# One V quad beside each group of four K slots across sequence-pair boundaries, with the last rows' R, the transposing reads and the first bundle rearranged

## The chip, the cores and the metric

The kernel runs on 1 core of one Trainium2 chip. The metric is the device time of one execution in microseconds (us); lower is better. Most runs below were made in rounds, in which the kernel under test and the kernel before take turns on the same chip.

## The reference

A causal convolution with softmaxed taps feeds a channel mix with a gate:

```python
x = conv(x, softmax(weight))            # 8 x 4160 x 192, 7 taps, 8 heads of 24 channels
x_prev = x shifted by one token
xk = mu_k * x + (1 - mu_k) * x_prev
xr = mu_r * x + (1 - mu_r) * x_prev
k  = relu(xk @ w_k)                     # 192 -> 1024
v  = (k * k) @ w_v                      # 1024 -> 192
out = sigmoid(xr @ w_r) * v             # 192 -> 192 for the gate
```

## The kernel before

Two sequences at a time (a "pair", four in all) go through the same pipeline. Tokens are cut into steps of 512 and a tail of 64 (4160 = 8 x 512 + 64). A step's K product is eight "slots" of one PSUM tile each. Four slots are a "bundle", the unit of the main loop; the tail is a bundle of one slot. A "quad" is four 128-token tiles of V (or of R, the gate). All PSUM tiles come from one ring of four, so each new tile waits for the fourth one back to be read out.

```python
ring = ctx.enter_context(tc.tile_pool(name="ring", bufs=4, space=bass.MemoryType.PSUM))
...
quads = []                                   # (step, quad, bundle in which its V runs)
for s, (p, t0, L, n0, ns) in enumerate(steps):
    for j in range(max(1, L // 256)):
        quads.append((s, j, last_bundle[s] + 1 + j + (s == 0 or L == TAIL and p < NPAIR - 1)))
...
def v_tail(s):                               # R and V of a tail, in the two banks of one tile
    ps = ring.tile([P, 2, BANK], FP32, tag="k", name="ps_vt")
    r_mm(ps[:, 1, 0:D], s, 0)
    r_sb = two.tile([P, D], BF16, tag="r_tail", name="r_tail")
    nc.scalar.activation(out=r_sb, in_=ps[:, 1, 0:D], func=AF.Sigmoid)
    v_mm(ps[:, 0, 0:D], s, 0)
    nc.vector.tensor_tensor(out=o_sb, in0=ps[:, 0, 0:D], in1=r_sb, op=ALU.mult)
    ...
# schedule of convolutions, writes of y, transposing reads and x loads (g: group of token blocks)
    xs = range(fb - 9, fb - 9 + nx)          # convolutions of pairs 1 to 3
    at(late, xs[-1], y_write, g)
    at(late, xs[-1] + (1 if g == 4 else 2), y_read, g)      # transposing read, DRAM -> yT
    b = {4: 1, 5: 1, 6: 2, 7: 9, 8: 11, 9: 14}.get(g)       # x loads, on the GpSimd queue
    b = first_bundle[first_step[p]] + (-16, -12, -6, -3)[(g - 6) % 4] if b is None else b
    at(early, b, load_x, g)
...
for b in range(quads[-1][2] + 1):            # the main loop
    ns = bundles[b] if b < len(bundles) else ()
    run(early, b)
    if ns: k_section(ns)                     # K matmuls, TensorE
    for n in ns: k_relu(n)                   # relu, ScalarE
    run(first, b)                            # transposes on TensorE, pair 0 only
    run(vq, b)                               # V quads, TensorE
    run(mixes, b)                            # d, xk, xr, VectorE
    for n in ns[:3]: k_square(n)             # VectorE
    run(vo, b)                               # o_sb = V * R, VectorE; output
    run(xt, b)                               # convolution and its casts, R and its sigmoid, tails
    for n in ns[3:]: k_square(n)
    run(late, b)                             # y writes, transposing reads, on the SP queue
```

## Time and profile before

The kernel before took 466.4 to 469.4 us in the four runs beside which the change was first timed (median 466.45). In the list of engines, "busy" is a share of the whole span. In a timeline each row is: start in us, duration in us, engine, line of the kernel, operation, output and inputs, shapes, count, and in brackets how long the engine had been idle and what ended that. The chain that ended last, from the page of the kernel before, by engine:

```profile
PE 64%; DMA 8%; DVE 5%; ACT 3%; issue 2%; SPq 0%; DVEq 0%; ACTq 0%
```

Two thirds of it is TensorE; the rest is work that TensorE had to wait for, and DMA is the largest part of that rest. The profile also records the clock granted to TensorE; a "half-clock window" below is a stretch in which that record shows half the full clock (in the kernel before 3.41 us from 253.7 us). A "read" is a transposing read of y from DRAM, an "x load" a load of the input, issued by GpSimd.

### The profile page before, as it was taken

Reading aid. Unit: us, or ns where it says so; the run is one execution under the profiler, and the core shown is the slowest. Engines: PE = TensorE matmul, PEld = TensorE weight load, DVE = VectorE, ACT = ScalarE, POOL = GpSimd, SP = SyncE. Lnnn points to the kernel's source line nnn. Section 1 sums busy time; section 2 is a strip of 40 time slices with the busy share of each in tenths; the row PEclk is TensorE's granted clock in tenths of the full one; section 3 lists DMA queues with packets and bytes.
Section 4 is the critical chain, followed back from the end, with each engine's and each line's share of the span. In section 5 each row is a group of like instructions: output and inputs, shape, how many; then the busy total and the mean of one; then the engine's idle time right before and its main releaser. Section 6 shows DMA issues by size and latency. Waiting matters only on the chain.

```text
span 464.4 us, 9771 instructions
## 1 busy us (share of the span) xinstructions
PE 437.4 (94%) x3940; PEld 305.1 (66%) x3940; DVE 388.3 (84%) x699; ACT 354.1 (76%) x465; POOL 48.1 (10%) x70
## 2 busy tenths in 40 slices
PE   7789999899897999999987999999989799999996
PEld 3465776576755666676665666776666566677775
DVE  5799789788877899888877789889987799899982
ACT  3778888688757887888857778789886787777772
POOL 8550001012002010010202010001200000000000
PEclk9999999999999999999999999999999999999998
DMA  7998745995699596357948749359476456331123
GB/s 92 154 167 159 182 125 132 148 203 144 123 188 132 149 183 160 101 85 189 187 118 176 135 130 214 89 92 199 124 134 163 108 149 149 110 99 53 58 69 112
DMA packets 133183, 63.64 MB, mean 137 GB/s; under 512 B 84722, under 2 KB 132882, under 8 KB 133138
## 3 DMA queue, kind: packets, MB, share of 16 engines
q1 hardware_dynamic: 94834, 48.28, 40.5%
q0 software_dynamic: 38224, 14.68, 28.0%
q8 instruction: 31, 0.51, 0.4%
q14 instruction: 14, 0.11, 0.1%
q10 hardware_dynamic: 80, 0.05, 0.0%
HBM read 29.39 MB, written 36.99 MB: 143 GB/s over the span
## 4 chain that ended last, share of the span: by engine, by line
PE 64%; DMA 8%; DVE 5%; ACT 3%; issue 2%; SPq 0%; DVEq 0%; ACTq 0%
PE ps_v L488 28%; PE ps_k L406 27%; DMA yT<-y_dram 6%; PE ps_r L484 3%; PE ps_r L483 3%; DMA xb<-in_x_dram 2%; PE ps_c L250 2%; ACT k_sb L446 2%; DVE k L465 2%; DVE o_sb L515 1%; PE ps_vt L488 1%; DVE d L345 1%; DVE xk L384 1%; DVE xk L387 0%; PE ps_k L434 0%
## 5 line engine op out<-in xcount | busy, mean ns | idle before, releaser
L446 ACT ACTIVATE k_sb<-ps_k 128x1024 bf16<-128x1024 f32 x260 | 245.7, 1033 | 19.0 <-PE ps_k L406 12.3
L406 PE MATMUL ps_k<-xk,wk 64*128 64x512 bf16 (+3 forms) x1056 | 192.3, 375 | 5.7 <-DVE xk L387 2.1
L488 PE MATMUL ps_v<-wv,k 128*128 128x192 bf16 x2048 | 179.4, 246 | 3.4 <-DVE o_sb L515 2.8
L488 PEld LDWEIGHTS <-k 128*128 128x128 bf16 x2048 | 170.7, 98 | 17.2 <-issue 3.7
L465 DVE TENSOR_TENSOR k<-k_sb 128x1024 bf16<-128x1024 bf16 x256 | 168.6, 686 | 12.3 <-ACT k_sb L446 11.1
L406 PEld LDWEIGHTS <-wk 64*128 64x128 bf16 (+1 forms) x1056 | 66.7, 96 | 107.1 <-issue 60.8
L515 DVE TENSOR_TENSOR o_sb<-ps_v,r_sb 128x768 f32<-128x768 f32 x64 | 61.2, 957 | 31.6 <-PE ps_v L488 31.6
L505 ACT ACTIVATE r_sb<-ps_r 128x768 bf16<-128x768 f32 x64 | 52.9, 828 | 28.0 <-PE ps_r L484 28.0
L286 ACT CAST y<-ps_c 120x480 bf16<-120x480 f32 (+6 forms) x84 | 38.6, 521 | 41.4 <-PE ps_c L250 41.4
L122 POOL DMA_DIRECT2D xb<-in_x_dram x36 | 32.2, 899 | 178.4 <-PE ps_k L406 98.6
L483 PE MATMUL ps_r<-wr,xr 128*128 128x192 bf16 x256 | 47.8, 248 | 0.3 <-ACT k_sb L446 0.3
L484 PE MATMUL ps_r<-wr,xr 128*128 128x192 bf16 x256 | 47.9, 248 | 0.0
L387 DVE TENSOR_TENSOR xr<-xr,yT 128x1024 bf16<-128x1024 bf16 (+1 forms) x66 | 36.2, 549 | 2.3
L387 DVE TENSOR_TENSOR xk<-xk,yT 128x1024 bf16<-128x1024 bf16 (+1 forms) x66 | 36.2, 549 | 2.3
L345 DVE TENSOR_TENSOR d<-yT 128x1536 bf16<-128x1536 bf16 (+2 forms) x37 | 31.6, 854 | 6.8 <-DMA yT<-y_dram 6.7
L250 PE MATMUL ps_c<-xb,toe 128*128 128x480 bf16 (+4 forms) x144 | 31.6, 322 | 1.6 <-DVE toe L224 0.9
L384 DVE TENSOR_SCALAR xk<-d,mu 128x1024 bf16<-128x1024 bf16 (+1 forms) x66 | 28.2, 427 | 1.2
L484 PEld LDWEIGHTS <-xr 128*128 128x128 bf16 x256 | 25.2, 98 | 4.1 <-issue 0.5
L289 ACT CAST y<-ps_c 120x480 bf16<-120x480 f32 (+6 forms) x45 | 20.7, 508 | 8.9 <-PE ps_c L250 8.9
L483 PEld LDWEIGHTS <-xr 128*128 128x128 bf16 x256 | 25.1, 98 | 3.6
L384 DVE TENSOR_SCALAR xr<-d,mu 128x1024 bf16<-128x1024 bf16 (+1 forms) x66 | 26.9, 408 | 0.0
L250 PEld LDWEIGHTS <-toe 128*128 128x128 bf16 x144 | 12.8, 98 | 4.4 <-DVE toe L224 1.6
(57 smaller groups left out, 79.6 us busy)
## 6 DMA issues: line engine op xcount, KB each, us to landing
out_dram<-o_sb SPq DMA_DIRECT2D x62, 384.0 KB, 2.9
y_dram<-y SPq DMA_DIRECT2D x10, 900.0 KB, 7.3
xb<-in_x_dram POOLq DMA_DIRECT2D x14, 480.0 KB, 8.4
xb<-in_x_dram POOLq DMA_DIRECT2D x6, 432.0 KB, 7.6
xb<-in_x_dram POOLq DMA_DIRECT2D x10, 192.0 KB, 6.3
y_dram<-y SPq DMA_DIRECT2D x3, 450.0 KB, 4.1
y_dram<-y SPq DMA_DIRECT2D x1, 810.0 KB, 6.3
xb<-in_x_dram POOLq DMA_DIRECT2D x2, 384.0 KB, 7.0
```

The source lines that it names most:

```text
L250: nc.tensor.matmul(out=ps[:, :, :, i * G : (i + 1) * G], lhsT=toe[:, h, :], rhs=xbs[g][:, :nb, :, h * G : (h + 1) * G], start=True, stop=True,
L286: copy(out=yh[:, :, :, c0 : c0 + n], in_=ps[:BLK, :, :, 0:n])
L384: nc.vector.tensor_scalar(out=o, in0=d[:, sl, :L], scalar1=mu[:, i, part : part + 1], scalar2=None, op0=ALU.mult)
L387: nc.vector.tensor_tensor(out=o, in0=o, in1=yT[:, sl, c0 : c0 + L], op=ALU.add)
L406: nc.tensor.matmul(out=ps[:, i, f * L : (f + 1) * L], lhsT=wk[r, 0 if hi else 1, fs], rhs=xk[r, i if hi else 2, :L], start=start and f == ...
L446: nc.scalar.activation(out=k_sb, in_=ps.rearrange("p a b -> p (a b)"), func=AF.Relu)
L465: nc.vector.tensor_tensor(out=o, in0=i, in1=i, op=ALU.mult)
L483: nc.tensor.matmul(out=o, lhsT=hi, rhs=wr[:, 0, :], start=True, stop=False)
L484: nc.tensor.matmul(out=o, lhsT=lo, rhs=wlo, start=False, stop=True)
L488: nc.tensor.matmul(out=o, lhsT=k2s[s][:, f, t * P : (t + 1) * P], rhs=wv[:, f, :], start=(f == 0), stop=(f == NF - 1),)
L505: nc.scalar.activation(out=r_sbs[s, j], in_=ps, func=AF.Sigmoid)
L515: nc.vector.tensor_tensor(out=o_sb.rearrange("p (b t) d -> p b (t d)", b=2), in0=v_ps.pop((s, j)), in1=r_sbs.pop((s, j)), op=ALU.mult,)
```

## The change

The intent: where one pair hands over to the next, give each group of four K slots one V quad again, so that the evictions of K on ScalarE and the products on VectorE stay spread out. The tail's R moves a bundle ahead of its V. The transposing reads (and what feeds them) come one bundle sooner, and the first bundle runs in two halves so that the transposes for the second step start sooner.

```diff
@@ k_section: works for a part of a bundle
+        h = len(ns) // 2
-        for n in ns[:2]:            (hi and lo halves of the first two slots, then of the others)
+        for n in ns[:h]:
...
@@ where each V quad goes
     quads = []
+    vb = 1
     for s, (p, t0, L, n0, ns) in enumerate(steps):
-        for j in range(max(1, L // 256)):
-            quads.append((s, j, last_bundle[s] + 1 + j + (s == 0 or L == TAIL and p < NPAIR - 1)))
+        for j in range(L // 256):
+            vb = max(vb, last_bundle[s]) + 1
+            if p < NPAIR - 1 and vb < len(bundles) and len(bundles[vb]) == 1:
+                vb += 1
+            quads.append((s, j, vb))
+        if L == TAIL:
+            quads.append((s, 0, vb))
@@ the tail's R, a tile of its own
+    def r_tail(s):
+        ps = ring.tile([P, 2, BANK], FP32, tag="k", name="ps_rt")
+        r_mm(ps[:, 0, 0:D], s, 0)
+        r_sbs[s, 0] = two.tile([P, D], BF16, tag="r_tail", name="r_tail")
+        nc.scalar.activation(out=r_sbs[s, 0], in_=ps[:, 0, 0:D], func=AF.Sigmoid)
...
+            at(xt, vb - 1, r_tail, s)
             at(xt, vb, v_tail, s)
@@ convolutions, writes, reads and x loads of pairs 1 to 3
-            xs = range(fb - 9, fb - 9 + nx)
+            xs = range(fb - 10, fb - 10 + nx)
-            b = {4: 1, 5: 1, 6: 2, 7: 9, 8: 11, 9: 14}.get(g)
-            b = first_bundle[first_step[p]] + (-16, -12, -6, -3)[(g - 6) % 4] if b is None else b
+            b = {4: 1, 5: 1, 6: 2, 7: 5, 8: 10, 9: 13}.get(g)
+            b = first_bundle[first_step[p]] + (-17, -13, -7, -4)[(g - 6) % 4] if b is None else b
@@ main loop: bundle 0 in halves
-            if ns:
-                k_section(ns)
-            for n in ns:
-                k_relu(n)
-            run(first, b)
+            for part in (ns[:2], ns[2:]) if b == 0 else (ns,):
+                if part:
+                    k_section(part)
+                for n in part:
+                    k_relu(n)
+                if part[:1] == ns[:1]:
+                    run(first, b)
```

More of the change, by code (lines that the diff above doesn't have):

```diff
@@ L418, in k_section @@
             return k_mm_tail(ns[0], steps[s][0])
-        for n in ns[:2]:
+        h = len(ns) // 2
+        for n in ns[:h]:
             k_mm(n, True, True)
-        for n in ns[:2]:
+        for n in ns[:h]:
             k_mm(n, False, False)
-        for n in ns[2:]:
+        for n in ns[h:]:
             k_mm(n, False, True)
-        for n in ns[2:]:
+        for n in ns[h:]:
             k_mm(n, True, False)
@@ L531, in v_tail @@
         ps = ring.tile([P, 2, BANK], FP32, tag="k", name="ps_vt")
-        r_mm(ps[:, 1, 0:D], s, 0)
-        r_sb = two.tile([P, D], BF16, tag="r_tail", name="r_tail")
-        nc.scalar.activation(out=r_sb, in_=ps[:, 1, 0:D], func=AF.Sigmoid)
         v_mm(ps[:, 0, 0:D], s, 0)
         o_sb = two.tile([P, D], FP32, tag="o_tail", name="o_tail")
-        nc.vector.tensor_tensor(out=o_sb, in0=ps[:, 0, 0:D], in1=r_sb, op=ALU.mult)
+        nc.vector.tensor_tensor(out=o_sb, in0=ps[:, 0, 0:D], in1=r_sbs.pop((s, 0)), op=ALU.mult)
         for i in range(2):
```

## The prediction

> **What bounds the kernel now.** I read the page first, for the busy shares and the clock.
>
> ```profile
> PE 437.4 (94%) x3940; PEld 305.1 (66%) x3940; DVE 388.3 (84%) x699; ACT 354.1 (76%) x465; POOL 48.1 (10%) x70
> PEclk9999999999999999999999999999999999999998
> ```
>
> TensorE leads, VectorE is ten points behind, and the clock is nearly whole. Then the timeline of TensorE alone, to see whether there are gaps and where. A plain bundle, here one of pair 0:
>
> ```profile
> 97.20 2.96 PE L406 MATMUL ps_k<-xk,wk 128*128 128x512 bf16 x16
> 100.00 2.80 PE L488 MATMUL ps_v<-wv,k 128*128 128x192 bf16 x32
> 102.64 0.57 PE L250 MATMUL ps_c<-xb,toe 128*128 128x480 bf16 x2
> ...
> 103.70 2.96 PE L406 MATMUL ps_k<-xk,wk 128*128 128x512 bf16 x16
> ```
>
> By its starts a bundle is K 2.80, V 2.64, convolution 0.41, R 0.66 us: 6.50 us without a gap. Here only less TensorE work would help, and the change removes none. The gaps lie elsewhere: at the start, in one bundle near 90 us, and at the three places where one pair of sequences hands over to the next. The first hand-over, from the last full bundle of pair 0 to the second step of pair 1:
>
> ```profile
> 116.72 3.00 PE L406 MATMUL ps_k<-xk,wk 128*128 128x256 bf16 x32
> 119.55 2.80 PE L488 MATMUL ps_v<-wv,k 128*128 128x192 bf16 x32
> ...
> 125.42 1.07 PE L434 MATMUL ps_k<-tail,wk 128*128 128x128 bf16 x16 [1.34 <-DVE o_sb L515]
> 126.32 5.44 PE L488 MATMUL ps_v<-wv,k 128*128 128x192 bf16 x64
> 131.60 0.57 PE L250 MATMUL ps_c<-xb,toe 128*128 128x480 bf16 x2
> 132.00 2.96 PE L406 MATMUL ps_k<-xk,wk 128*128 128x512 bf16 x16
> ...
> 138.13 1.36 PE L406 MATMUL ps_k<-xk,wk 64*128 64x512 bf16 x6 [0.48 <-ACT y L286]
> ...
> 143.02 0.82 PE L488 MATMUL ps_vt<-wv,k2t 128*128 128x192 bf16 x8 [2.72 <-ACT r_tail L534]
> ...
> 144.34 2.97 PE L406 MATMUL ps_k<-xk,wk 128*128 128x512 bf16 x16
> ```
>
> Two V quads run back to back beside the tiny tail K, then eight K slots come with no V beside them. Eight evictions of about 1 us on ScalarE then cannot hide behind 5.6 us of K. The list of waits shows which of these repeat:
>
> ```profile
> PE ps_vt L488 <- ACT r_tail L534: 8.6, 4, 2.7
> DVE d L345 <- DMA yT<-y_dram: 6.7, 4, 2.8
> ```
>
> Three r_tail waits are 2.72 us each: the tail's R is issued, its sigmoid queues on ScalarE behind four relus and the casts, and the tail's V stands behind it.
>
> Last, the timeline around the second hand-over and at the start:
>
> ```profile
> 20.12 2.98 PE L406 MATMUL ps_k<-xk,wk 128*128 128x512 bf16 x16 [2.14 <-DVE xk L387]
> ...
> 231.25 0.96 DVE L345 TENSOR_TENSOR d<-yT 128x1536 bf16<-128x1536 bf16 x1 [2.02 <-DMA yT<-y_dram]
> ...
> 236.92 2.84 PE L488 MATMUL ps_v<-wv,k 128*128 128x192 bf16 x32 [1.57 <-DVE o_sb L515]
> ...
> 254.72 4.12 PE L406 MATMUL ps_k<-xk,wk 128*128 128x512 bf16 x16
> ```
>
> The late transposing read delays d on VectorE, so the product that frees V's PSUM tile is late, and TensorE waits 1.57 us. The K after the r_tail gap took 4.12 us instead of 2.97.
>
> [...]its clock record has one half-clock window of 3.41 us from 253.7 us, right after the second r_tail gap, and none after the other two, which have the same gap. [...]r_tail's sigmoid, ready near 140.3, starts at 142.47 after casts emitted before it. [...]the transposing read issued at 50.08 with no x load behind it landed after 6.7 us; those at 76.03, 110.80, 221.87 and 333.42, each with an x load issued about 1 us later, landed after 9.4, 8.9, 9.4 and 9.0 us.
>
> **Part 1, V quads and the tail's R across hand-overs.** Nothing is added or removed; one VectorE/ScalarE instruction each way at most. Computing the new lists by hand: the tail's bundle gets no V, the next two bundles of the new pair get one V each, and V of the tail follows in the second, with its R already in the first. TensorE's work from the K of the last full bundle to the K four bundles on is three bundles with convolution, 3 x 6.50 = 19.5, plus tail K 0.90, one more convolution 0.41, tail R 0.16, tail V 0.66: 21.6 us. Measured by starts, the three hand-overs take 144.34 - 116.72 = 27.6, 254.72 - 227.79 = 26.9, 365.43 - 339.34 = 26.1 us. Idle: 6.0 + 5.3 + 4.5 = 15.8 us. The half-clock K adds 4.12 - 2.97 = 1.15, not inside these. So 16.9 us is the most that can be won here.
>
> What stays. In the new order the first thing in the tail's bundle that needs V's PSUM tile is an R, 2.83 + 2.64 + 0.41 + 0.90 + 0.41 = 7.2 us after the K. VectorE ends that product in the first hand-over at 125.36, 8.6 us after K, of which 0.28 was a DMA wait: 8.4 - 7.2 = 1.2 us stay. That bundle carries four mixing groups (two steps and a tail) on VectorE. In the second: 236.86 - 2.02 - 227.79 = 7.05; in the third the same: nothing stays. ScalarE in the last full bundle and the tail's bundle has 3.77 + 1.02 + 1.02 + 1.02 + 0.83 = 7.7 us against TensorE's 7.9, and its sigmoid then sits just before the fourth K slot of the next bundle: I leave 0.7 us there in the second and third, 0.1 in the first. Residue 1.3 + 0.7 + 0.7 = 2.7. Gain 16.9 - 2.7 = **14.2 us**.
>
> **Part 2, everything for the transpose a bundle sooner.** Convolution, write, read and x loads of pairs 1 to 3 all move by one bundle (some 6.5 us), so the waits of 0.28, 2.02 and 1.65 us on the hand-over reads go; that is already in part 1. The first x load of pair 1 moves from bundle 9 to 5: it leaves the side of the read in bundle 8 (d waited 2.80 us, TensorE 2.06 at 91.13) and comes to stand beside the read of bundle 4. By the landing times above that read becomes 9.4 instead of 6.7 us, 59.5 instead of 56.8; d started at 57.03, so it waits about 2.4, and 0.26 of slack follows. TensorE waits about 2.0 near 63 instead of 2.06 near 91. Net **0.3 us** won.
>
> **Part 3, first bundle in halves.** The transposes for step 1 come after two K slots instead of four, so 1.4 us sooner by 2.9/2 of K. VectorE's chain from there (copies, d, mix) is what K at 20.12 waits for (2.14 us), and ScalarE, busy without a gap from 21.53 to 31.8, starts as much sooner. The halves now take one slot after the other with two more switches between 128 and 64 rows: **1.2 us** won.
>
> **Part 4, the end.** The last tail's V waits 0.42 us for its sigmoid; now gone: **0.4 us**.
>
> Sum: 14.2 + 0.3 + 1.2 + 0.4 = 16.1. I keep back 0.4 for small waits not listed. 466.5 - 15.7 = **450.8 us**, 3.4% less.
>
> **Rivals.** (a) VectorE takes over at the hand-overs. Its work there is, in the first, some 8.4 + 0.7 + 5.6 + 7.1 = 21.8 us (from the rows of d, xk, xr, square 0.69, product 0.96), as much as TensorE's 21.6; in the others 7.1 + 0.7 + 5.6 + 7.1 = 20.5. For it: these are sums without waits[...]. Against: it comes out of the last bundle only 0.7 us late. It would cost 1 to 1.5 us more per hand-over: about 455. (b) The ring of four PSUM tiles: R of the tail now takes its own tile, and the fourth K slot behind it waits for its sigmoid. ScalarE in that bundle has 3.77 + 1.02 + 0.83 + 0.45 = 6.1 against TensorE's 6.7. If it lags, 0.5 each: 452. (c) The moved x load: if the read beside it lands later still, or the early bundles, where ScalarE is full, lose what the halves win: 452.5. (d) All waits vanish: 466.5 - 18.5 = 448.
>
> **Range and chances.** The gain of part 1 is bounded above by counted idle time, below by (a) with (b) and (c) together, about 456. I say 447.5 to 455.5. The 2% line is at 457.4; to miss it more than 40% of the idle must come back. Faster 0.90, within 2% 0.09, slower 0.01.
>
> **What the new profile should show.** No V wait on r_tail; K starts four bundles apart at hand-overs 22 to 23 us; first hand-over slowest, an R waiting about 1 us for a product; no half-clock window there; d waiting for a transposing read once, near 57 to 60 us, followed by a K wait near 62; K of the second bundle near 18.9 instead of 20.12; plain bundles still 6.1 to 6.5. I am wrong if plain bundles lengthen, or if VectorE shows waits of over 2 us on TensorE at each hand-over while V sits in order.

## The result, and the profile after

The changed kernel took 449.63, 456.72, 450.66 and 455.44 us: median 453.05. The ratio to the kernel before is 0.9676, 95% interval 0.9597 to 0.9755: faster. A ratio here is the mean time of one kernel's fast runs over that of the other's fast runs of the same rounds, so it is not quite the ratio of the medians. The profile fell on the 449.63 us run. Busy shares and the chain, from its page:

```profile
PE 430.4 (96%) x3877; PEld 304.4 (68%) x3940; DVE 387.9 (87%) x699; ACT 354.1 (79%) x465; POOL 48.2 (11%) x70
...
PE 81%; DVE 8%; ACT 4%; DMA 4%; issue 2%; SPq 0%; DVEq 0%; ACTq 0%
```

The work is the same (VectorE, ScalarE and the weight loads within 1 us; 63 matmul records are missing from this trace, so its PE time reads low). The chain is now 81% TensorE instead of 64%. The first hand-over on TensorE, from its timeline:

```profile
115.14 3.00 PE L406 MATMUL ps_k<-xk,wk 128*128 128x256 bf16 x32
117.97 2.80 PE L495 MATMUL ps_v<-wv,k 128*128 128x192 bf16 x32
...
121.01 1.06 PE L435 MATMUL ps_k<-tail,wk 128*128 128x128 bf16 x16
...
123.53 0.24 PE L490 MATMUL ps_r<-wr,xr 128*128 128x192 bf16 x1 [1.05 <-DVE o_sb L522]
...
126.99 2.80 PE L495 MATMUL ps_v<-wv,k 128*128 128x192 bf16 x32
...
136.78 0.82 PE L495 MATMUL ps_vt<-wv,k2t 128*128 128x192 bf16 x8
...
138.10 2.96 PE L406 MATMUL ps_k<-xk,wk 128*128 128x512 bf16 x15
```

From K to K it takes 138.10 - 115.14 = 22.96 us, where it took 27.62. The 2.72 us wait of the tail's V is gone, and one wait is left: an R for the product of the last V. The other two hand-overs take 21.99 and 21.98 us with no wait that the timeline marks. The second bundle's K, from the same timeline:

```profile
18.88 2.98 PE L406 MATMUL ps_k<-xk,wk 128*128 128x512 bf16 x15 [1.13 <-DVE xk L387]
```

It was at 20.12 with a 2.14 us wait. And in bundle 6 and 7, from the timelines of VectorE and TensorE:

```profile
57.52 0.96 DVE L345 TENSOR_TENSOR d<-yT 128x1536 bf16<-128x1536 bf16 x1 [1.66 <-DMA yT<-y_dram]
...
63.19 2.53 PE L406 MATMUL ps_k<-xk,wk 128*128 128x512 bf16 x14 [1.21 <-DVE o_sb L522]
```

It comes in place of one in the kernel before:

```profile
91.13 2.53 PE L406 MATMUL ps_k<-xk,wk 128*128 128x512 bf16 x14 [2.06 <-DVE o_sb L515]
```

That one belonged to the read in bundle 8, beside which the x load stood before; the new one belongs to the read in bundle 4, beside which it stands now. One more thing is new, and the profile of one run cannot show it: the runs fall into two sets, near 450 and near 455 to 457 us. The first set is what the prediction worked out; many of the experiments went into the second.

### The profile page after: what moved, and what is told of

The parts are those of the page before. It is cut to its first block, busy times and chain, and to the rows that moved or that the text cites. A ratio compares the mean times of both kernels' runs of the same rounds, so it can differ in the third digit from the quotient of the medians.

```text
span 447.8 us, 9705 instructions
## 1 busy us (share of the span) xinstructions
PE 430.4 (96%) x3877; PEld 304.4 (68%) x3940; DVE 387.9 (87%) x699; ACT 354.1 (79%) x465; POOL 48.2 (11%) x70
## 4 chain that ended last, share of the span: by engine, by line
PE 81%; DVE 8%; ACT 4%; DMA 4%; issue 2%; SPq 0%; DVEq 0%; ACTq 0%
PE ps_v L495 35%; PE ps_k L406 34%; PE ps_r L490 4%; PE ps_r L491 4%; PE ps_c L250 4%; DMA yT<-y_dram 4%; DVE k L466 2%; ACT y L286 2%; DVE o_sb L522 1%; ACT k_sb L447 1%; DVE d L345 1%; DVE xk L387 1%; DMA w_raw<-in_weight_dram 1%; DVE xk L384 1%; ACT y L289 1%
## 5 line engine op out<-in xcount | busy, mean ns | idle before, releaser
L406 PE MATMUL ps_k<-xk,wk 64*128 64x512 bf16 (+3 forms) x994 | 187.7, 373 | 7.3 <-DVE o_sb L522 1.6
L495 PEld LDWEIGHTS <-k 128*128 128x128 bf16 x2048 | 170.9, 98 | 14.9 <-issue 0.7
L250 PEld LDWEIGHTS <-toe 128*128 128x128 bf16 x144 | 12.7, 98 | 2.9 <-DVE toe L224 1.5
```

What stands on the lines that cost most here:

```text
L250: nc.tensor.matmul(out=ps[:, :, :, i * G : (i + 1) * G], lhsT=toe[:, h, :], rhs=xbs[g][:, :nb, :, h * G : (h + 1) * G], start=True, stop=True,
L406: nc.tensor.matmul(out=ps[:, i, f * L : (f + 1) * L], lhsT=wk[r, 0 if hi else 1, fs], rhs=xk[r, i if hi else 2, :L], start=start and f == ...
L495: nc.tensor.matmul(out=o, lhsT=k2s[s][:, f, t * P : (t + 1) * P], rhs=wv[:, f, :], start=(f == 0), stop=(f == NF - 1),)
```

## The experiments

Each experiment tells what it changes against the changed kernel, or against the kernel named. The "quiet" runs are those near the fastest; the runs of the second set are called slow here. The record has a state "slow" of its own, for runs over 1.5% above the fastest of their kernel; it falls on some runs of the second set only (456.72 in the first rounds, 458.34 in again, 456.83 in tail_xr, three in no_halves), and the ratios leave those out. All results were correct. Twelve kernels ran, on four chips, and the kernel before itself ran from 463.1 to 472.1 us beside them, so small differences are read from runs of one call or from the traces.

### The two sets of runs: again, no_halves, load_b6, tail_xr

These four ran in one call on one chip. **again** is the changed kernel without an edit.

> The changed kernel itself once more, because its four runs went from 449.6 to 456.7 us where those of the kernel before lie within 0.2 us but for one. I expect 449.5 to 456.8 again, two or three of the runs near 450 and the others near 455. Theory V1 (half-clock windows[...]): a slow run has a granted clock some 0.004 to 0.008 under 0.998. Theory V2 (data for the first bundles comes late in some runs): slow runs may have the full clock and a long wait of a convolution or of K in the first 40 us.

Measured: 449.36, 456.05, 456.06, 458.34, 450.12, 449.96 us; ratio 0.9667 (0.9598 to 0.9736). The spread is real and as expected; the profile fell on a quiet run. Two of the slow runs, 456.05 and 456.06 us, had a granted clock of 0.995. Over their 454 us that is at most 2.3 us of lost clock (an estimate from these two numbers), and they are some 6 us longer than the quiet ones: the clock alone can't make the second set.

**no_halves:**

```diff
-            for part in (ns[:2], ns[2:]) if b == 0 else (ns,):
+            for part in (ns,):
```

> The changed kernel with the first bundle whole again. Undoing the halves should cost 1.2 us beside a fast run of the changed kernel: 450.8 to 451.0 us, with the K of the second bundle near 20.1 us again. On the spread: V2 says that the halves brought the kernel closer to the x loads of the start (a convolution waits 0.25 us for its load at 22.7 us, which it did not before), so without them the runs should lie within 1 us; V1 says the spread stays as wide as with them.

Measured: 450.60, 454.85, 458.80, 459.04, 458.21, 455.81 us; ratio 0.9775 (0.9719 to 0.9831), unclear at 2%. Its quietest run is 1.2 us over that of again. The spread stays, so theory V2 (late data at the start, brought on by the halves) falls.

**load_b6:**

```diff
-            b = {4: 1, 5: 1, 6: 2, 7: 5, 8: 10, 9: 13}.get(g)
+            b = {4: 1, 5: 1, 6: 2, 7: 6, 8: 10, 9: 13}.get(g)
```

> The first x load of pair 1 in bundle 6 instead of 5, away from the transposing reads of bundles 4 and 8. My theory says the x load beside a read makes it land 2.2 to 2.7 us later: then the wait of K at 63.2 us (1.21 us) goes and nothing comes at 89: 448.3 to 448.6 us fast. The rival, that the read of bundle 4 is late of itself (writes of y and other traffic), leaves the 1.2 us wait where it is: 449.6.

Measured: 448.40, 449.13, 448.51, 448.92, 448.39, 448.72 us; ratio 0.959 (0.9545 to 0.9634). One number moved, and the second set of runs is gone. The K wait at 63 us is gone too. VectorE's d, which waited 1.66 us for the read in the changed kernel, now shows no wait:

```profile
55.76 0.96 DVE L345 TENSOR_TENSOR d<-yT 128x1536 bf16<-128x1536 bf16 x1
```

So the x load in bundle 5 makes the slow runs, and V1 (clock windows alone, at random) falls as their main cause.

**tail_xr:**

```diff
-        rb = fb - 1 if L == TAIL else fb
+        rb = fb - 1 if L == TAIL and p == NPAIR - 1 else fb
```

> The mixing of the tail's xr (three VectorE operations, 0.83 us) in the tail's own bundle instead of the one before, for pairs 0 to 2. My theory: R in the first hand-over waits 1.05 us because VectorE has too much in the bundle before the tail, so 0.8 of it goes: 448.8 us fast, the other two hand-overs unchanged. Rival: the product there waits for V or for a relu, then nothing changes: 449.6.

Measured: 454.95, 449.47, 449.46, 456.83, 449.53, 455.67 us; ratio 0.9657 (0.959 to 0.9724). Here the profile fell on a slow run (454.95 us; the record's state is fast). Its timelines of VectorE and TensorE in bundles 6 and 7:

```profile
61.53 0.96 DVE L345 TENSOR_TENSOR d<-yT 128x1536 bf16<-128x1536 bf16 x1 [5.82 <-DMA yT<-y_dram]
...
63.81 0.60 PE L406 MATMUL ps_k<-xk,wk 128*128 128x512 bf16 x2 [2.20 <-DVE xk L387]
...
67.20 3.37 PE L406 MATMUL ps_k<-xk,wk 128*128 128x512 bf16 x11 [2.79 <-DVE o_sb L522]
```

The transposing read came 4 us later than in the quiet trace (5.82 us of wait against 1.66), TensorE waits twice, and the clock record shows 6.8 us of half clock from 65.0 us. The parts of DMA issued between 48 and 66 us, with the time from issue to landing at the end of the line, first for the quiet changed kernel:

```profile
xb<-in_x_dram POOLq DMA_DIRECT2D x2, 480.0 KB, 9.4
yT<-y_dram SPq DMA_TRANSPOSE x1, 8.7
```

and for the slow run of tail_xr:

```profile
xb<-in_x_dram POOLq DMA_DIRECT2D x2, 480.0 KB, 11.6
yT<-y_dram SPq DMA_TRANSPOSE x1, 12.8
```

and for load_b6, where the x load comes a bundle later:

```profile
xb<-in_x_dram POOLq DMA_DIRECT2D x2, 480.0 KB, 6.6
yT<-y_dram SPq DMA_TRANSPOSE x1, 6.2
```

Counting the DMA packets of the traces by the microsecond in which they end shows what happens in between (256-byte packets belong to the read, 384-byte packets to the x load):

```
us                     50   51   52   53   54   55   56   57   58   59   60   61
changed, quiet  read    6 1012  995 1134  374   71    8    0    0    0    0    0
                x       0    0    0    0  306  444  491  492  504  261   62    0
tail_xr, slow   read  155  866  533  223  273  280  275  285  278  276  155    1
                x       0    0  122  219  272  272  270  275  275  279  255  191
```

In both, the read is issued at 48.7 to 48.8 us and the x load 0.64 us behind it. In the quiet run the x packets begin at 54, when the read is nearly done. In the slow run they begin at 52, and from then on the read gets some 280 packets a microsecond instead of 1000 to 1130. There read and x load end nearly the same number of packets in each microsecond from 54 to 59 (273 to 285 against 270 to 279), though a packet of the one is 256 bytes and of the other 384.

As to the tail's xr: in this trace the first hand-over takes 143.44 - 121.34 = 22.10 us instead of 22.96, as expected, but the three quiet runs are hardly faster than those of again (449.49 against 449.81 us on average, where 0.8 was expected). Whether the quiet runs waited longer at the read is not known, since none was profiled; **best** below settles the part about xr.

### The overlap made certain: load_b4

```diff
-            at(early, b, x_tile, g, nc.vector)
-            at(early, b, load_x, g)
+            tb, b = (xt, 4) if g == 7 else (early, b)
+            at(tb, b, x_tile, g, nc.vector)
+            at(tb, b, load_x, g)
```

> The changed kernel with the first x load issued about two us sooner, just before the transposing read of bundle 4 instead of just behind it. If slow runs come from x packets starting while that read is still running, nearly every run should now be slow: the read's packets take about 10 us instead of 5.3, d waits 4 to 6 us, 454 to 458 us, no run near 450. Rival (the spread is chance in the memory or the clock and not this overlap): the same mix as before, with some runs near 450.

Measured: 457.87, 455.57, 457.03, 455.73, 457.87, 459.15 us; ratio 0.9804 (0.9763 to 0.9846), unclear at 2%. All six runs are slow. The edit did less than intended: GpSimd still waited and issued the load only 0.04 us behind the read instead of 0.64. That was enough: the x packets begin at 51.3 us, ahead of the read's at 52.5. VectorE's timeline, and the DMA issued between 48 and 66 us:

```profile
63.16 0.96 DVE L345 TENSOR_TENSOR d<-yT 128x1536 bf16<-128x1536 bf16 x1 [6.97 <-DMA yT<-y_dram]
```

```profile
yT<-y_dram SPq DMA_TRANSPOSE x1, 14.0
```

So the overlap is the cause of the second set: all six runs are slow where it is made certain, none where the load is moved away. (No slow run of the changed kernel without an edit was profiled; that its slow runs are like the one of tail_xr is inferred.)

In this case much goes with how close behind the read the x load is issued. In the traces there are four reads with an x load issued 0.04 to 0.34 us behind them, this one and three in b6_old_quads below; in all four the x packets start inside the read (here even ahead of its first packet), which then lands after 10.8 to 17.4 us. At 0.64 us, where the change put the first x load, they do so in one profiled run of four (tail_xr; not in those of the changed kernel, again and no_halves). At 0.66 to 2.4 us, some 90 reads in the 14 profiles, they never start more than 1.3 us before 95% of the read's packets have ended.

What remains open is why, with the same issue times, the x packets start at 52 in one run and at 54 in another; no run here tests a cause.

### The same move in the kernel before: before_b6

```diff
-            b = {4: 1, 5: 1, 6: 2, 7: 9, 8: 11, 9: 14}.get(g)      (in the kernel before)
+            b = {4: 1, 5: 1, 6: 2, 7: 6, 8: 11, 9: 14}.get(g)
```

> The kernel before with one number changed: the first x load of pair 1 in bundle 6 instead of 9, so that it stands beside no transposing read. Theory (x packets that start while the read is still running slow it, and how early they start varies from run to run): the 2.06 us K wait near 91 us goes, 464.2 us where the kernel before has 466.4; its runs still spread by 2 to 6 us, because the reads at its hand-overs, with an x load behind each, have no slack (d waits 0.28, 2.02 and 1.65 us even in a quiet run). Rival, that only the read in bundle 8 varies: all runs within 1 us.

Measured: 462.54 to 466.03 us, median 464.79 in 12 runs; the kernel before beside it 463.55 to 472.13. Ratio 0.9951 (0.9924 to 0.9978): the same at 2%. In the trace the bundle that took 8.73 us (88.47 to 97.20) takes 6.67, so the 2.06 us of the theory are there. The spread narrows from 5.3 us (the fast runs; 8.6 with one run in the record's slow state) to 3.5. The profiled run (465.18 us) has half-clock windows at 20.7 and 252.8 us; the bundles in which they fall take 0.9 and 1.1 us more than in traces without. In the kernel before the time goes with the clock: over the runs beside all the experiments, six with a granted clock of 1.000 took 463.1 to 464.1 us, eleven with 0.985 took 468.4 to 470.0 us. So such windows may well make up its spread, and a read that varies, as in the theory, is not shown for it; no experiment tells the two apart.

### The parts one by one, from load_b6

With the disturbance gone, the parts can be undone singly. The reference point is load_b6: 448.62 us, spread 0.7. Hand-overs are K to K as above.

**b6_old_quads** (V quads by the old formula; the tail's R still ahead, the reads still early):

```diff
-        for j in range(L // 256):
-            vb = max(vb, last_bundle[s]) + 1
-            ...
+        for j in range(max(1, L // 256)):
+            quads.append((s, j, last_bundle[s] + 1 + j + (s == 0 or L == TAIL and p < NPAIR - 1)))
```

> From load_b6, V quads placed as before (two V beside the tail's K), while the tail's R stays a bundle ahead and the reads stay early. My prediction put all of the hand-over gain in one sum. Splitting it: of the idle 6.0 + 5.3 + 4.5 us of before, the tail's sigmoid makes 2.9 each, late reads 0.3, 1.6 and 1.2; left for the V order are 2.8, 0.8 and 0.4, against 1.4, 0.4 and 0.4 that load_b6 still has. So 448.6 + 1.8 = 450.4 us. Rival, that the V order carries most of the gain, as the name of the change says: 455 or more.

Measured: 453.69, 454.57, 453.45, 455.33, 453.93 us; ratio 0.9718 (0.9676 to 0.976). The order of V is worth 5.3 us, not the 1.8 I had split off. TensorE at the first hand-over:

```profile
123.56 5.44 PE L489 MATMUL ps_v<-wv,k 128*128 128x192 bf16 x64
129.25 2.96 PE L406 MATMUL ps_k<-xk,wk 128*128 128x512 bf16 x16
133.54 0.59 PE L406 MATMUL ps_k<-xk,wk 128*128 128x512 bf16 x2 [0.59 <-ACT k_sb L447]
...
137.51 0.82 PE L489 MATMUL ps_vt<-wv,k2t 128*128 128x192 bf16 x8
```

Eight K slots without a V run into the relus (at 133.54), as the prediction read it from the kernel before. The hand-overs take 25.08, 22.54 and 22.54 us (load_b6: 22.97, 21.98, 21.99), together 3.2 us more, and the bundles behind them lose another 1.1, 0.3 and 0.3. The remaining 0.3 us is at the start of the profiled run, where a convolution waited 1.31 us for its x load (0.38 in load_b6), and is no part of the change. The loss behind the hand-overs was in none of my sums: I had counted only up to the fourth K. And 0.8 of the 1.1 us is not the V order itself: the old order also moved the x loads closer behind the reads, the read issued at 131.01 landed after 17.4 us with an x load 0.29 us behind it, d waited 1.53 us for it, and the K at 154.08 waited for the product behind d. That leaves some 4.2 us for the V order.

**b6_r_beside** (the tail's R back beside its V, in one tile; the edit puts back `v_tail` as it was and takes `r_tail` away):

> From load_b6, the tail's R back beside its V, in one PSUM tile, V quads and reads as in the changed kernel. Theory: the tail's V waits for the sigmoid, which is emitted behind four relus and two casts in its bundle; ScalarE reaches it some 8.0 us after the K of the bundle where TensorE is there at 6.1, so about 2 us for each of three hand-overs and 0.4 at the end: 448.6 + 6.4 = 455 us, up to 457 if half-clock windows follow the gaps. Rival: with V spread over the bundles ScalarE is less behind, so the wait shrinks below 1 us: 451.

Measured: 451.75, 451.89, 452.75, 451.95, 451.98 us; ratio 0.9697 (0.9661 to 0.9732). It costs 3.3 us, half of what was expected:

```profile
136.89 0.82 PE L495 MATMUL ps_vt<-wv,k2t 128*128 128x192 bf16 x8 [1.18 <-ACT r_tail L541]
```

With a V in the bundle, TensorE comes to the tail later and ScalarE is less behind, so the wait is 1.18 us instead of 2.72, and no half-clock window follows (the profiled run's granted clock is 1.000). Three hand-overs cost 1.26 to 1.28 us each, 3.8 in all; at the end 0.4 is won back (see the point on the end below).

**b6_r_own** (as b6_r_beside, R and V of the tail in two PSUM tiles):

```diff
-        ps = ring.tile([P, 2, BANK], FP32, tag="k", name="ps_vt")
-        r_mm(ps[:, 1, 0:D], s, 0)
+        ps_r = ring.tile([P, 2, BANK], FP32, tag="k", name="ps_rt")
+        r_mm(ps_r[:, 1, 0:D], s, 0)
...
+        ps = ring.tile([P, 2, BANK], FP32, tag="k", name="ps_vt")
         v_mm(ps[:, 0, 0:D], s, 0)
```

> As b6_r_beside (the tail's R in the bundle of its V), but with R and V of the tail in two PSUM tiles instead of the two banks of one. If the 1.18 us wait of the tail's V for the sigmoid comes only from sharing a tile, it goes: 448.6 to 449.2 us, and moving R a bundle ahead was not needed for that. Rival: the next tile of the ring then waits for the same sigmoid and the wait only changes its place: 451 to 452.

Measured: 448.08 to 449.02 us, median 448.26 in 6 runs; ratio 0.9591 (0.9558 to 0.9624). The wait came from sharing a tile: V and R use different banks, but in one tile the tail's V waited 1.18 us for the sigmoid (b6_r_beside), and with two tiles its row shows no wait (135.61 us). In the new order a second tile would have done as well as moving R a bundle ahead.

**b6_late** (convolutions, writes, reads and x loads of pairs 1 to 3 a bundle later, as before; the first x load stays in bundle 6):

```diff
-            xs = range(fb - 10, fb - 10 + nx)
+            xs = range(fb - 9, fb - 9 + nx)
-            b = {4: 1, 5: 1, 6: 2, 7: 6, 8: 10, 9: 13}.get(g)
+            b = {4: 1, 5: 1, 6: 2, 7: 6, 8: 11, 9: 14}.get(g)
-            ... (-17, -13, -7, -4) ...
+            ... (-16, -12, -6, -3) ...
```

> From load_b6, convolutions, writes, reads and x loads of pairs 1 to 3 a bundle later, as before (only the first x load stays in bundle 6). Theory: d waits for the read again by 0.3, 2.0 and 1.6 us at the hand-overs and the R in the tail's bundle waits about as much for the product: 448.6 + 3.7 = 452.3 us, with a wider spread than 0.7 us, since a disturbed read has no slack. Rival: the new order has slack elsewhere and hides the late read: 449.

Measured: 450.99, 451.32, 450.91, 450.68, 451.38 us; ratio 0.9675 (0.964 to 0.9711). It costs 2.4 us. The R in the tail's bundle waits in all three hand-overs, first here:

```profile
122.50 0.24 PE L490 MATMUL ps_r<-wr,xr 128*128 128x192 bf16 x1 [1.48 <-DVE o_sb L522]
```

then 1.30 and 1.09 us (load_b6: 1.05, none, none). The expected wider spread did not come: the runs lie within 0.7 us. So these reads are not disturbed in the way that the one in bundle 4 is, although an x load is issued 0.67 to 0.92 us behind seven of them: in the profiled run its packets begin 4.0 to 5.3 us later, as the read's last packets end.

**b6_no_halves** (first bundle whole again, the edit of no_halves):

> From load_b6, first bundle whole again. 448.6 + 1.2 = 449.8 us, and now without the wide spread of no_halves, since the disturbed read is out of the way: all runs within 1 us. If V2 of before had some truth, the spread would differ from load_b6's 0.7 us.

Measured: 450.52, 449.35, 450.84, 450.84 us; ratio 0.9634 (0.9592 to 0.9675). It costs 2.1 us, not 1.2. The K of the second bundle, first of this kernel, then of load_b6:

```profile
19.97 4.54 PE L406 MATMUL ps_k<-xk,wk 128*128 128x512 bf16 x16 [2.15 <-DVE xk L387]
```

```profile
18.84 2.98 PE L406 MATMUL ps_k<-xk,wk 128*128 128x512 bf16 x16 [1.13 <-DVE xk L387]
```

At the end of the 2.15 us wait a half-clock window of 3.4 us began (19.9 to 23.3 us in the clock record), and K took 4.54 instead of 2.98 us. The run of 449.35 us fits one without such a window (its granted clock was 0.997, that of the other three 0.994), but it was not profiled.

### Both mends: best

The edits of load_b6 and tail_xr together.

> Both mends together: x load in bundle 6 and the tail's xr in the tail's own bundle. In the trace of tail_xr the first hand-over took 143.44 - 121.34 = 22.10 us against 22.96 in the changed kernel, so on top of the 448.6 of load_b6 this should give 447.8 us, all runs within 1 us. Rival, that the 0.86 comes back later (VectorE falls behind in the new pair): 448.6.

Measured: 447.65, 447.80, 447.95, 447.51 us; ratio 0.9577 (0.9537 to 0.9617). It has the lowest median of the study, 5.3 us under the changed kernel's median in its first rounds. The R in the first hand-over:

```profile
121.67 0.24 PE L490 MATMUL ps_r<-wr,xr 128*128 128x192 bf16 x1 [0.18 <-DVE o_sb L522]
```

The wait went from 1.05 to 0.18 us, which shows that VectorE's load before the tail made it.

## Why the prediction was right, and where not

**The total** was predicted as 450.8 us, range 447.5 to 455.5; measured 453.05. The quiet runs (449.36 to 450.66) lie 0.1 to 1.4 under the number, the disturbed ones (454.85 and up in the kernels with this read and load together) 4 us and more above it. The median of four lies between the two sets, where no run fell; with one more slow run among the four it would have been some 455 us or more, at the edge of the range. That it lies so near the number is in part luck; that the quiet runs do is not.

**Part 1, hand-overs, right in sum.** Predicted 14.2 us; the three hand-overs went from 27.62 + 26.93 + 26.09 to 22.96 + 21.99 + 21.98 us, 13.7, and the slow K of 4.12 us went with its half-clock window, 1.15: 14.9. The residue was put at 1.3 + 0.7 + 0.7 and is 1.3 + 0.4 + 0.4. The 1.2 us wait of an R for VectorE in the first hand-over came as 1.05. The wait of a fourth K slot for a sigmoid, for which 0.7 was left, showed only as a K of 3.23 instead of 2.96 us. Two readings in it were loose. The tail's V did not stand behind the sigmoid by order alone: b6_r_own shows that in the new order the wait is gone when R and V don't share a PSUM tile (1.18 us in b6_r_beside). And the half-clock window (3.41 us) was counted as going with the tail's gap: it did come right after a gap of 2.72 us, but only one of three equal gaps had one, so what brings it on is not shown.

**Part 2, the moved x load, right in place and wrong in kind.** The prediction said that the wait at 91 us would go and one near 63 would come, and both happened. The step that failed is the landing time: "By the landing times above that read becomes 9.4 instead of 6.7 us". It took the landing times of one trace and treated them as fixed. The traces show two outcomes: 8.7 us when the x packets start as the read ends, 12.8 when they start inside it (14.0 when they start ahead of it). In the first case the K wait is 1.21 us, not the 2.0 foreseen, so this part won some 0.85 us instead of 0.3; the second costs some 4 to 9 us in K waits and half-clock windows. In the kernel before this load was issued 0.70 us behind the read in bundle 8; its one trace shows no early start there, so whether the change moved the risk or brought it in is not shown. My rival (c) named this but gave it only 1.7 us.

**Part 3, the halves, right, and larger at times.** 1.2 us predicted; K started 1.24 us sooner (20.12 to 18.88), as the transposes did (16.01 to 14.77). By its starts the first part of K took 1.57 us, 0.16 more than half of the 2.83 of the whole; whether the two more switches make that is not shown. In b6_no_halves undoing it cost 2.1; there the longer wait (2.15 us) was followed by a half-clock window of 3.4 us, in which K took 4.54 instead of 2.98 us.

**Part 4, the end, wrong in sign.** The 0.42 us wait of the last tail's V did go. But from the last tail's K to the end of the span it takes 447.8 - 435.12 = 12.7 us, where it took 464.4 - 452.10 = 12.3. The last tail's output on the SP queue, first of the kernel before, then of the changed one (DMA issued in the last 9 us, with the time from issue to landing):

```profile
out_dram<-o_tail SPq DMA_DIRECT2D x1, 48.0 KB, 2.0
```

```profile
out_dram<-o_tail SPq DMA_DIRECT2D x1, 48.0 KB, 2.9
```

The last full V starts 0.17 us later (the tail's R is now ahead of it), and the tail's output follows closer on the last 384 KB output and takes 0.9 us longer. b6_r_beside, where R is beside V, ends in 450.03 - 437.76 = 12.3 us. In the four traces the landing goes with the pause before the tail's output on the SP queue: 2.0 us behind a pause of 0.44 (before) and 0.45 us (b6_r_beside), 2.9 behind one of 0.09 us (the changed kernel and b6_r_own, which has R beside V). So 0.4 us were lost, not won.

**Rivals.** (a), VectorE as the bound, holds only for the 1.05 us of the first hand-over, and tail_xr and best show that it was VectorE's load. (b) did not come. (d), no waits at all, would be 448; best reached 447.7 by removing the two that were left.

**What each part is worth** from load_b6, by undoing it: V order 5.3 (with the 0.8 of a late read and the 0.3 at the start), tail's R 3.3 (or a second PSUM tile), earlier reads 2.4, halves 2.1: 13.1 us. load_b6 ran on another chip than these; the spans of the profiled runs give 5.3, 3.4, 2.7 and 2.2 us. From before_b6 to load_b6 it is 464.79 - 448.62 = 16.2, also on different chips. The parts need not add up, since one wait can hide another; in the kernel before, the tail's R alone waited 2.72 us three times, which b6_r_beside puts at 1.18.

## What to carry to other kernels

Count the work between two like points of the pipeline and compare it with the time between them: at these hand-overs this gave the gain to within 1 us before anything was built, but look also at the bundles behind the gap, where another 1.7 us lay (0.8 of it a late read). When a transfer that the critical path needs has another one issued right behind it, treat its landing time as a distribution and not as a number (here 8.7 us in the quiet trace and 12.8 in the slow one, both with the x load 0.64 us behind): time the kernel several times, and move the second transfer before explaining the first one's mean. And look at what a wait is set on: a second PSUM tile for the tail's gate did as much as moving it a bundle ahead (448.26 against 448.62 us).

## What the traces show of the clock and the DMA

- A half-clock window came with an idle time of 2.15 us (b6_no_halves, K of 4.54 instead of 2.98 us) and one of 2.72 us (the kernel before, 4.12 instead of 2.97). The same gap of 2.72 us at two other hand-overs had none.
- The read of 3600 packets in bundle 4 landed in 6.2 us with no x load beside it (load_b6), in 8.7 with an x load's packets right behind it, and in 12.8 (tail_xr) to 14.0 (load_b4) with them inside it; in tail_xr it then got some 280 instead of 1000 to 1130 packets a microsecond.
- For the first x load of pair 1 the traces show, from the start of the issuing instruction to the first packet, 1.7 us with no read beside it (load_b6, 56.40 to 58.06), and 2.1 to 4.7 us with one issued 0.04 to 0.64 us ahead of it (49.20 to 51.28 in load_b4, 49.31 to 52.1 in tail_xr, 49.47 to 54.12 in the changed kernel).
